# Attention, routed experts and FFN on one core: constants built behind the first pair's loads, attention rows stored pair by pair, and a newly searched order of steps

## The chip, the cores and the metric

The kernel runs on one core of a Trainium2 chip. The metric is the device time of one execution in microseconds (us), lower is better. A core has five engines with a queue each: TensorE (PE, its weight loads shown as PEld), VectorE (DVE), ScalarE (ACT), GpSimd (POOL) and SyncE (SP). An engine runs its own queue strictly in order and waits at an instruction until what that instruction needs is there. SP computes nothing: it only issues transfers (DMA) between the memory of the chip (DRAM here) and the core's memory, and an issue that waits holds up all later ones in its queue. ACT and POOL can issue transfers too. Matmul results go to PSUM, in banks of 128 x 512 numbers; tiles there and in the core's memory come from pools with a fixed number of buffers for each tag, so that a new tile may have to wait until an older one has been read.

## What is computed

```python
# q, k, v: 4 batches x 8 heads x 576 tokens x 64, float32
local = softmax(causal(q @ k.T / 8)) @ v
q_p = where(q > 0, q, exp(q) - 1) + 1
mem_out = (q_p @ M_prev) / (q_p @ z_prev + 1e-6)
g = 1 / (1 + exp(-beta))                       # one number for each head
x = (g * mem_out + (1 - g) * local)            # -> 2304 tokens x 512
...
e = argmax(x @ w_gate)                         # one expert of 8 for each token
y = softmax(x @ w_gate)[e] * sigmoid(x @ w_output_gate)[e] * (relu(x @ w1[e]) @ w2[e])
...
h = y @ w_in
out = (h - tanh(h)) @ w_out                    # 512 -> 2048 -> 512
```

## The kernel before, in words

The program has three stages, one after the other: attention, the routed experts (`run_slots`), and the FFN (`ffn`). The change touches the first stage and the point where it hands over to the second; the code of the other two is the same.

**Attention** works on 16 *pairs*: four batches `b` times four pairs of heads `hp`, numbered `n = 4b + hp`. One pair takes this course, and each step is one `add(...)` of the function `pair`:

- SP loads k (`kr`), q (`qr`) and v (`vr`, with the last 64 rows in `vt`), several transfers each. The last 64 rows of q and of k share one block of the tile `qr`.
- PE turns k and q over (`tk`, `tq`, `tt`), and ACT or DVE copies the results out of PSUM (`kt`, `qt`; DVE makes `qtt`).
- PE makes the scores of four blocks of query rows (`sc0` makes two of them, `sc2`, `sc3`, each with one matmul for each head), and of the last 64 rows of both heads together (`sct`, and `sdt` for its last 64 columns). DVE masks each block and takes its extreme (`mx`, `mxt`), ACT takes the exponential (`ex`, `ext`).
- PE turns the results over (`g0`, `g1`, `g2`, `ta`, `tb`), ACT or DVE copies them (`cp`, `ca`, `cb`) into `att`.
- Beside that, ACT, POOL and DVE make the memory branch: `qexp`, `qmin` (POOL), `phi`, `pz` (POOL, with `z`), `gn`, and after the sums are known `nrm` and `p` (POOL). PE turns `p` over (`tp`, `tpt`).
- PE multiplies with v (`av0`, `av1`, `av2`, 20 matmuls into `l`) and adds the memory part (`avM`, with `M`). The result is copied (`lt`), and one more matmul (`xo`, with the constant `w160`) turns it back and makes the columns for the experts' choice on the way. DVE scales it into `xb` (`xw`).

After the last pair of a batch, DVE sums the choice columns (`acc`), and the **router** (class `Router`) finds each token's expert in about thirty small steps; PE's part of it is the group `rank`, which writes `rp` from `ohb`. The rows of `xb` go to the DRAM table `xd` in five transfers (`putx`), the gate factors `sc` in two more (`puts`). In the second stage experts fetch their tokens from `xd` by index. After the third batch one expert's first slot is already fetched (`e_gather`) and turned over (`e_xt`), so that the second stage can begin at once.

**The order of work** is not written by hand. `Plan.add` collects all steps with a cost for each engine and a due time out of the table `DUE` (plus the pair's number times `PERIOD`). `Plan.order` walks through them: among the steps whose inputs are planned and whose buffers are free it takes the one due first, and with its model of costs gives it a time. The steps are emitted in that order, and since each engine runs in order, it is the order on every engine. If a step issues several instructions on several engines, all of them go in at that place, whether its cost names them or not.

**Constants.** Before the plan starts, `make_consts0`, `Router.__init__` and `make_consts` emit the identity `idf`, the masks, the gate factors from `beta` (`g`, `gt`, `ft`), `w160`, zeros for `att`, `vt` and `M`, and the router's small tables: for these POOL writes numbers (`iota`) into one shared buffer `io`, and DVE turns them into floats (`CAST`, L707, L723, L728), one after the other.

Of the kernel before, what the change touches and what calls it, by code (L numbers as in the profile page):

```python
# [57 lines left out]
def make_consts0(tc, pool):  # L58
    nc = tc.nc
    c = Consts()  # L60
    c.idf = pool.tile([P, P], F32, name="idf")
    make_identity(nc, c.idf)

    c.tri = pool.tile([P, P], BF16, name="tri")
    nc.gpsimd.memset(c.tri, 1.0)
    nc.gpsimd.affine_select(out=c.tri, in_=c.tri, compare_op=ALU.is_gt, fill=0.0,
                            base=0, pattern=[[1, P]], channel_multiplier=-1)
    c.ones = pool.tile([P, P], BF16, name="ones")
    nc.gpsimd.memset(c.ones, 1.0)
    return c  # L70


def make_consts(tc, c, pool, beta, w_gate, w_ogate):

    nc = tc.nc

    def tile1(name, shape, dt=F32):
        return pool.tile(shape, dt, bufs=1, name=name)


    c.cm = tile1("cm", [P, 512 + P])
# [8 lines left out]
    nc.gpsimd.memset(c.bm, 0.0)  # L90
    c.sel = tile1("sel", [P, P])
    for j in range(2):
        pr = slice(D * j, D * j + D)
        nc.gpsimd.memset(c.bm[pr, j:j + 1], 1.0)
        nc.vector.tensor_tensor(out=c.sel[:, pr], in0=c.idf[:, 0:D], in1=c.idf[:, D:P], op=ALU.add)


    g0, g, f = (tile1(n, [P, H]) for n in ("g0", "g", "f"))
    nc.sync.dma_start(g0, beta.unsqueeze(0).to_broadcast([P, H]))
# [9 lines left out]
    c.gt = tile1("gt", [P, NPAIR, NT, 2])  # L109
    c.ft = tile1("ft", [P, NPAIR, NT, 2])  # L110
# [4 lines left out]
    c.w160 = tile1("w160", [P, NPAIR, 2, 80])  # L115
# [28 lines left out]
class Plan:  # L144

# [37 lines left out]
    def order(self):  # L183
# [19 lines left out]
        while ready:  # L203
# [60 lines left out]
PERIOD = 23.73  # L264
ROUTE = 1.78
DUE = {
    "pz": (-91.5,), "qexp": (-84.8,), "qt": (-84.8,), "ptt": (-84.4,),
    "mx": (-59.4, -1.4, -5.0, -2.9, -31.8, -33.8, 16.5, -30.4), "ca": (-58.7, -10.0), "qmin": (-34.1,),
    "ex": (-33.6, 17.3, -4.6, 12.5, 16.0, -2.3, 26.1, 20.7), "loadq": (-30.6,), "consts": (-30.0,),
    "kt": (-26.7,), "loadk": (-22.3,), "qtt": (-11.6,), "sct": (-10.5,), "tp": (-10.5,), "phi": (-10.1,),  # L270
    "nrm": (-6.2,), "new": (-4.8,), "mxt": (-3.4,), "ktt": (-2.6,), "avM": (-1.5,), "mv": (0.7,), "tk": (0.7,),
# [5 lines left out]
}  # L277


def attention(tc, c, pl, ps, src, M_prev, z_prev, rt):  # L280
# [17 lines left out]
    def consts(b):  # L298
        def f(e):
            z = pl.tile([P, H * D], F32, tag="z", name=f"z_{b}")  # L300
            nc.sync.dma_start(z, z_prev[b].rearrange("h d -> (h d)").unsqueeze(0).to_broadcast([P, H * D]))
            state.z = {**getattr(state, "z", {}), b: z}
            for j in range(2):
                pr = slice(D * j, D * j + D)
                nc.sync.dma_start(c.M[b % 2][pr, :, pr], M_prev[b].rearrange("(n j) d e -> j d n e", j=2)[j])
        plan.add(b * NPAIR * PERIOD + DUE["consts"][0], f"consts_{b}", (("SP", 0.3),), f,
                 w=[f"z{b}", f"M{b % 2}"], new=[("z", f"z{b}")], lat=4.0)

    def pair(b, hp):
# [12 lines left out]
        def load(name):  # L322
# [13 lines left out]
            add("load" + name, (("SP", 0.4),), f, w=w, new=[(name + "r", K(name + "r"))], lat=5.0)  # L336
# [24 lines left out]
        add("gn", (("DVE", 1.2),), gn, r=[K("pz")], w=[K("gn")])  # L361
# [237 lines left out]
        add("xo", (("PE", 3 * mm(160) + 0.1),), xo(0), r=[K("lt/a"), K("lt/b")], w=[K("xo")], new=[("tr", K("xo"))])  # L599
# [14 lines left out]
        add("xw", (("DVE", 0.46),), xw(1), r=[K("l0"), K("r")], w=[f"xb{b % 2}/{hp}1"])  # L614

    def batch(b):
# [21 lines left out]
        for k, (t, name, f) in enumerate(sorted(rt.batch(b, accs.get, pl, ps), key=lambda x: x[0])):  # L638
# [5 lines left out]
            dur = {"hot": 1.7, "e_gather": 1.2, "e_sc0": 1.2, "e_sc1": 1.2, "e_xt0": 0.44, "e_xt1": 0.44, "e_list": 0.6}.get(nm, 0.25 if eng != "SP" else 0.5)  # L644
            if nm == "put":
                eng = "ACT" if b == B - 1 else eng
                plan.add(base + DUE["r"][0], f"{name}_{b}", ((eng, 0.4),), lambda e, f=f: f(), r=xs, w=[f"xd{b}"], lat=6.0)
                continue
            r, w, new = [prev], [f"R{b}_{k}"], []
# [25 lines left out]
class Router:  # L675
# [3 lines left out]
    def __init__(self, tc, c, pool, xd):  # L679
# [6 lines left out]
        self.rank = pool.tile([P, n], F32, name="rank")  # L686
        nc.gpsimd.memset(self.cs[:, 0, :], 0.0)
# [31 lines left out]
        self.pt = pool.tile([P, n, 2], F32, name="ptc")  # L719
# [56 lines left out]
    def batch(self, b, get, pl, ps):  # L776
# [896 lines left out]
```

## Time and profile before

| what | us |
|---|---|
| three runs | 1007.35, 1006.24, 1007.66 |
| median | 1007.35 |
| the profiled execution's own time | 1006.93 |
| its span in the profile | 1005.1 |
| PE busy | 929.8 (93%) |
| DVE busy | 816.2 (81%) |
| ACT busy | 660.3 (66%) |
| POOL busy | 128.5 (13%) |

The span is the time from the first to the last instruction of the profiled execution; 1.8 us of its own time lie around it. Shares of busy time are averages over three stages that have different limits, so the rows below are read by stage: attention runs to about 282 us, the experts from there to about 580, the FFN to the end. The granted clock of TensorE (PEclk) is a share of its full speed, so 1.00 is 2.4 GHz and 0.50 is 1.2 GHz.

### The profile page before, as it was taken

What the parts mean: (1) busy time and instruction counts of PE and PEld (TensorE: products, weight loads), DVE (VectorE), ACT (ScalarE), POOL (GpSimd) and SP (SyncE); (2) the same over time, 40 slices, a digit from 0 to 9 for tenths busy, and PEclk for the clock granted to TensorE, in tenths of its full rate; (3) what the DMA queues carried; (4) which work ended last, traced back from release to release, by engine and by line L of the source; (5) the groups of instructions that cost most, each with busy time, mean ns of one, the idle gap of its engine ahead of it and who ended that gap; (6) DMA issues with size and microseconds to landing.
All of it is one profiled execution on the core that took longest, in us unless ns stands there. A gap on an engine that the chain in (4) does not pass through costs nothing. (4 is left out here: it accounts for less than half of the span.)

```text
span 1005.1 us, 16594 instructions
## 1 busy us (share of the span) xinstructions
PE 929.8 (93%) x5661; PEld 760.2 (76%) x5661; DVE 816.2 (81%) x1901; ACT 660.3 (66%) x1448; POOL 128.5 (13%) x145
## 2 busy tenths in 40 slices
PE   3998998998959999999999979999999999999996
PEld 2565665665649998989989958777888788788885
DVE  4767675867659898998988869999888888888896
ACT  2777576776625667676687566767667666756684
POOL 4333222232221100001000000001000100100010
PEclk9999999999979999999999979999999999999999
DMA  5323324513176788798888410101000100100010
GB/s 115 79 53 72 89 46 83 124 32 77 35 215 213 250 280 268 256 297 248 276 289 283 135 44 22 43 1 43 1 0 1 43 1 1 43 1 0 4 41 21
DMA packets 138413, 103.60 MB, mean 103 GB/s; under 512 B 85072, under 2 KB 119888, under 8 KB 138320
## 3 DMA queue, kind: packets, MB, share of 16 engines
q1 hardware_dynamic: 130432, 90.70, 31.2%
q0 software_dynamic: 3200, 10.58, 3.2%
q10 hardware_dynamic: 4688, 1.18, 0.6%
q8 instruction: 46, 0.75, 0.3%
q14 instruction: 47, 0.39, 0.1%
HBM read 92.93 MB, written 9.51 MB: 102 GB/s over the span
## 5 line engine op out<-in xcount | busy, mean ns | idle before, releaser
L1440 PE MATMUL og<-wouth,fgl 128*128 128x512 f32 x288 | 115.4, 401 | 7.9 <-DVE fgl L1451 7.8
L1440 PE MATMUL og<-woutl,fgh 128*128 128x512 f32 x288 | 114.6, 398 | 0.0
L1440 PE MATMUL og<-wouth,fgh 128*128 128x512 f32 x288 | 113.4, 394 | 0.2
L1524 ACT ACTIVATE fu<-fph 128x512 f32<-128x512 f32 (+1 forms) x80 | 44.4, 555 | 105.4 <-PE fph L1491 77.6
L1491 PE MATMUL fph<-fxh,fwh 128*128 128x512 f32 (+1 forms) x256 | 94.2, 370 | 4.8 <-ACT fxh L50 4.8
L1491 PE MATMUL fph<-fxh,fwl 128*128 128x512 f32 (+1 forms) x256 | 93.5, 368 | 0.0
L1491 PE MATMUL fph<-fxl,fwh 128*128 128x512 f32 (+1 forms) x256 | 93.4, 367 | 0.0
L453 ACT ACTIVATE a<-a,nm 128x128 f32<-128x128 f32 (+3 forms) x128 | 72.6, 571 | 24.4 <-DVE nm L432 24.2
L1458 POOL DMA_INDIRECT out_dram<-ob,olist x18 | 18.9, 1048 | 459.8 <-ACT ob L1456 246.9
L1526 DVE SCALAR_TENSOR_TENSOR fs<-fs,fu 128x512 f32<-128x512 f32 (+1 forms) x80 | 50.9, 636 | 30.2 <-ACT fs L1525 29.8
L51 DVE TENSOR_TENSOR bl<-r,bh 128x512 fp32r<-128x512 f32 x96 | 64.5, 685 | 11.1 <-ACT bh L50 10.7
L1440 PEld LDWEIGHTS og<-wouth,fgl 128*128 128x128 f32 x288 | 54.2, 188 | 25.0 <-DVE fgl L1451 13.2
L1279 PE MATMUL y<-hh,bh 128*128 128x256 f32 x256 | 72.2, 282 | 0.0
L1279 PE MATMUL y<-hl,bh 128*128 128x256 f32 x256 | 71.6, 280 | 0.0
L1279 PE MATMUL y<-hh,bl 128*128 128x256 f32 x256 | 71.6, 280 | 0.0
L51 DVE TENSOR_TENSOR al<-r,ah 128x512 fp32r<-128x512 f32 x96 | 64.3, 684 | 0.1
L1440 PEld LDWEIGHTS og<-wouth,fgh 128*128 128x128 f32 x288 | 54.4, 189 | 12.6 <-ACT fgh L1446 1.5
L1440 PEld LDWEIGHTS og<-woutl,fgh 128*128 128x128 f32 x288 | 54.4, 189 | 12.0 <-DVE woutl L51 0.5
L432 DVE CUSTOM_DVE_ANT_0 a<-sc,cm 128x128 f32<-128x128 f32 (+3 forms) x128 | 55.5, 479 | 7.0 <-PE sc L412 6.9
L1537 DVE TENSOR_TENSOR ft<-fph,ft 128x512 f32<-128x512 f32 (+1 forms) x80 | 50.9, 636 | 11.6 <-ACT ft L1535 11.2
L1271 ACT ACTIVATE hh<-ph 128x256 fp32r<-128x256 f32 x64 | 24.6, 385 | 53.8 <-PE ph L1266 53.8
L1491 PEld LDWEIGHTS fph<-fxh,fwh 128*128 128x128 f32 x256 | 49.0, 192 | 14.1 <-ACT fxh L50 5.7
(372 smaller groups left out, 2825.2 us busy)
## 6 DMA issues: line engine op xcount, KB each, us to landing
r<-in_moe_w_dram SPq DMA_DIRECT2D x96, 512.0 KB, 5.0
d<-in_moe_w_in_dram SPq DMA_DIRECT2D x16, 512.0 KB, 4.6
d<-in_moe_w_out_dram SPq DMA_DIRECT2D x16, 512.0 KB, 4.4
qr<-in_q_dram SPq DMA_DIRECT2D x32, 128.0 KB, 2.7
kr<-in_k_dram SPq DMA_DIRECT2D x32, 128.0 KB, 2.6
vr<-in_v_dram SPq DMA_DIRECT2D x32, 128.0 KB, 2.6
r_e<-in_moe_w_dram SPq DMA_DIRECT2D x8, 512.0 KB, 5.8
xd<-xb SPq DMA_DIRECT2D x12, 256.0 KB, 4.2
```

The costliest lines, as they stand in the source:

```text
L51: nc.vector.tensor_tensor(out=lo, in0=src, in1=hi.bitcast(F32), op=ALU.subtract)
L432: nc.vector.tensor_tensor_reduce(out=y, in0=x, in1=mask, scale=-0.125, scalar=init, op0=ALU.add, op1=ALU.min, accum_out=out)
L453: nc.scalar.activation(a, a, AF.Exp, bias=s.nm[:, o:o + 1], scale=-1.0, accum_out=s.sum[:, i, j:j + 1])
L1271: nc.scalar.activation(hh, hv, AF.Relu)
L1279: nc.tensor.matmul(s.y[d // 2][:, d % 2, :], st[:, d * P:(d + 1) * P], mv, start=f == 0 and m == 0 and d % 2 == 0, stop=f == 7 and m == 2, ...
L1440: nc.tensor.matmul(og[ci][t], st[:, ts], mv, start=f == 0 and m == 0, stop=f == 15 and m == 2)
L1458: sc = nc.gpsimd.indirect_dma_start(out=out, out_offset=bass.IndirectOffsetOnAxis(ap=perm[:, i:i + 1], axis=0), in_=ob, in_offset=None).ins
L1491: nc.tensor.matmul(h, st[:, k, :], xp[ci, k][o], start=m == 0, stop=m == 11)
L1524: nc.scalar.activation(u, h, AF.Square)
L1526: nc.vector.scalar_tensor_tensor(out=s, in0=s, scalar=KA, in1=u, op0=ALU.add, op1=ALU.mult)
L1537: nc.vector.tensor_tensor(out=th, in0=h, in1=th, op=ALU.subtract)
```

## The change

- `make_consts` keeps what the first scores need. Four groups of constants become steps of the plan, with due times of their own (`DUE0`): `M` (zeros for the memory tiles), `zeros` (for `att` and `vt`), `gates` (from `beta`) and `w160`. The router's tables, with `tri` and `ones`, become a fifth step, `laterrt`, which calls `Router.consts`; its cost in the plan is 3.5 us of POOL. `beta` is loaded from ACT's queue instead of SP's.
- `z` and `M` of a batch are loaded by two steps instead of one.
- The rows of `xb` are stored by a step `put` of each pair: two transfers for the first 512 rows (one for each head), two for the last 64, all from SP's queue. The five transfers at the end of a batch go, those of the last batch (which ACT issued) among them.
- The plan's costs for loads change: 2.1, 1.15 and 1.75 us of SP for q, k and v where all had 0.4, and 3.0 us to land where it was 5.0. Its rule for PSUM banks changes by a line: any use of a bank now counts against all earlier ones from other engines.
- The due times are new.

```diff
 def make_consts0(tc, pool):
     c.tri = pool.tile([P, P], BF16, name="tri")
-    nc.gpsimd.memset(c.tri, 1.0)
-    nc.gpsimd.affine_select(out=c.tri, in_=c.tri, compare_op=ALU.is_gt, fill=0.0,
-                            base=0, pattern=[[1, P]], channel_multiplier=-1)
...
 def make_consts(tc, c, pool, beta, w_gate, w_ogate):
...
+    nc.scalar.dma_start(g0, beta.unsqueeze(0).to_broadcast([P, H]))
...
+    c.later = {
+        "M": lambda: memories(nc, c),
+        "zeros": lambda: zeros(nc, c),
+        "gates": lambda: gates(nc, c, g0, g, f),
+        "w160": lambda: columns(nc, c, w_gate, w_ogate),
+    }
...
 class Plan:
                 for k in touch[i][0] | touch[i][1]:
-                    t = max([t] + [u for g, u in wrote.get(k, {}).items() if g != e])
-                for k in touch[i][1]:
-                    t = max([t] + [u for g, u in read.get(k, {}).items() if g != e])
+                    t = max([t] + [u for d in (wrote, read) for g, u in d.get(k, {}).items() if g != e])
...
-PERIOD = 23.73
+PERIOD = 19.44
...
+DUE0 = {"constsM": 33.9, "constsz": 16.3, "laterM": -165.5, "latergates": 6.8, "laterrt": 17.1, "laterw160": -25.5, "laterzeros": 23.6}
...
 def attention(tc, c, pl, ps, src, M_prev, z_prev, rt):
+    for name, e, dur in (("M", "POOL", 1.1), ("zeros", "POOL", 0.9), ("gates", "DVE", 2.3), ("w160", "DVE", 0.9)):
+        plan.add(DUE0["later" + name], f"later{name}_0", ((e, dur),), lambda e, f=c.later[name]: f(), w=[f"later/{name}"],
+                 lat=6.0 if name == "w160" else 0.0)
+    plan.add(DUE0["laterrt"], "laterrt_0", (("POOL", 3.5),), lambda e: rt.consts(), w=["later/rt"], lat=1.0)
...
-            add("load" + name, (("SP", 0.4),), f, w=w, new=[(name + "r", K(name + "r"))], lat=5.0)
+            add("load" + name, (("SP", {"q": 2.1, "k": 1.15, "v": 1.75}[name]),), f, w=w, new=[(name + "r", K(name + "r"))], lat=3.0)
...
+        def put(e):
+            for r0, rows, x in ((b * S, 512, xb[:, 0:4, h0:h0 + 2, 0:D]), (b * S + 512, D, xb[0:D, 4:5, h0:h0 + 2, 0:D])):
+                for j in range(2):
+                    nc.sync.dma_start(rt.xd[r0:r0 + rows, h0 * D + j * D:h0 * D + j * D + D].rearrange("(t p) d -> p t d", t=x.shape[1]), x[:, :, j, :])
+        add("put", (("SP", 1.6),), put, r=[f"xb{b % 2}/{hp}0", f"xb{b % 2}/{hp}1"], w=[f"xd{b}{hp}"], lat=3.0)
...
 class Router:
-        at(0, "put")(lambda: putx(nc.scalar if b == B - 1 else nc.sync, get(b)[0]))
```

**Place 1, the head, queues of SP and DVE.** SP before, from its first transfer:

```order
L99 DMA g_157<-in_beta_dram 128x8
L329 DMA qr_215<-in_q_dram 128x4x64 x2
L333 DMA qr_215<-in_q_dram 64x2x64
L333 DMA qr_215<-in_k_dram 64x2x64
L301 DMA z_223<-in_z_prev_dram 128x512
L122 DMA w_181<-in_moe_w_gate_dram 64x4x8
L122 DMA w_181<-in_moe_w_output_gate_dram 64x4x8
L122 DMA w_181<-in_moe_w_gate_dram 64x4x8
L122 DMA w_181<-in_moe_w_output_gate_dram 64x4x8
L305 DMA M_205<-in_M_prev_dram 64x4x64 x2
L329 DMA kr_227<-in_k_dram 128x4x64 x2
L329 DMA qr_233<-in_q_dram 128x4x64 x2
```

and now (`w` is `w160`):

```order
L352 DMA qr_130<-in_q_dram 128x4x64 x2
L356 DMA qr_130<-in_q_dram 64x2x64
L356 DMA qr_130<-in_k_dram 64x2x64
L135 DMA w_109<-in_moe_w_gate_dram 64x4x8
L135 DMA w_109<-in_moe_w_output_gate_dram 64x4x8
L135 DMA w_109<-in_moe_w_gate_dram 64x4x8
L135 DMA w_109<-in_moe_w_output_gate_dram 64x4x8
L352 DMA kr_155<-in_k_dram 128x4x64 x2
L352 DMA qr_165<-in_q_dram 128x4x64 x2
```

The first k (`kr`) has lost `beta`, `z` and `M` ahead of it; `w160` still stands there. On DVE the router's tables stood ahead of the first block of scores (`a` and `nm` are written by `mx`):

```order
L707 CAST ish<-ish_i 128x20
L120 COPY w_181<-idf 64x64 x5
L707 CAST pos<-pos_i 128x20
L707 CAST thr<-thr_i 128x18
L347 SCALAR_TENSOR_TENSOR ph_220<-qr_215,ph_220 128x640
L723 CAST ptc<-io_t 128x40
L724 MEMSET ptc 64x4x2
L728 CAST ir<-io_r 128x128
L394 TENSOR_TENSOR qtt_265<-tt_263,bm 128x128
L432 ISA a_0_244,nm_241<-sc_0_268,cm 128x128
```

and now they stand between the last block of pair 0 and the first of pair 1:

```order
L383 RECIPROCAL gn_278<-gn_278 128x10
L735 CAST ie<-io_e 128x8
L738 TENSOR_SCALAR rev<-ie 128x8
L743 TENSOR_TENSOR le<-ie 128x64
L751 CAST num<-num_i 128x20
L751 CAST num_302<-num_i 128x20
L751 CAST ish<-ish_i 128x20
L751 CAST pos<-pos_i 128x20
L751 CAST thr<-thr_i 128x18
L766 CAST ptc<-io_t 128x40
L767 MEMSET ptc 64x4x2
L771 CAST ir<-io_r 128x128
```

The two instructions of DVE that follow are `phi` of pair 1, which needs POOL's `qmin` of pair 1, queued on POOL behind the router's tables, and the first `mx` of pair 1.

**Place 2, PE in the middle of a pair (here pair 5's scores).** Before, `sct` and then `sdt` (the matmul with 64 columns) followed `sc2`:

```order
L412 MATMUL sc_5_1080<-kt_1005,qt_1012 128x384
L412 MATMUL sc_5_1081<-kt_1005,qt_1012 128x384
L425 MATMUL sct_1086<-kt_1005,qtt_1038 128x512
L427 MATMUL sc_5_1081<-kt_1005,qtt_1038 128x64
L476 MATMUL g_4_1095<-idf,a_1_810 128x128 x4
```

Now `sdt` comes ahead of `sct`, and `tk` of the next pair has moved here:

```order
L435 MATMUL sc_5_1097<-kt_938,qt_868 128x384
L435 MATMUL sc_5_1098<-kt_938,qt_868 128x384
L450 MATMUL sc_5_1098<-kt_938,qtt_995 128x64
L448 MATMUL sct_1103<-kt_938,qtt_995 128x512
L391 MATMUL tk_1109<-idf,kr_1030 128x128 x4
```

The matmul with 64 columns writes into the bank of `sc2`'s second half; it now stands ahead of DVE's reading of that half instead of behind it.

**Place 3, PE at the turn of a batch (batch 0).** Before, the router's group `rp` (twelve instructions, of which the last two are shown) was followed by `xo`:

```order
L862 LDWEIGHTS ones
L862 MATMUL rp_1225<-ohb_1215,ones 128x8
L597 MATMUL xo_1243<-w_181,lt_1240 128x160 x3
L597 MATMUL l_4_1115<-w_181,lt_1240 128x160 x2
L377 MATMUL tt_1255<-idf,qr_965 128x128
```

Now the group (its first three instructions are shown) stands right behind the last matmuls of a pair with M, and `tq`, `ta` and `sc0` of other pairs follow it:

```order
L603 MATMUL l_5_1308<-pt_1316,M_116 128x128
L604 MATMUL l_5_1309<-pt_1316,M_116 128x448
L887 LDWEIGHTS tri
L887 MATMUL rp_1412<-ohb_1402,tri 128x40
L888 LDWEIGHTS ones
```

So `rp` no longer stands ahead of an `xo` that waits for `lt`, and waits for `ohb` at another point of DVE's work.

## Rows read from the trace of the kernel before

**Rows 1.** Busy time from the first to the last `av` of attention, by engine.

```profile
core 0: us, PE busy (x) PEld busy (x) DVE busy (x) ACT busy (x) POOL busy (x), PEclk, DMA share, GB/s
38.80:275.80 237.00, 219.25 (x1500) 147.45 (x1498) 164.64 (x621) 165.58 (x470) 67.69 (x51) 0.99 0.32 67
```

**Rows 2.** Timeline of the head: start us, us, engine, line, operation [idle before <-releaser].

```profile
3.64 0.17 DVE L101 TENSOR_SCALAR g<-g 128x8 f32<-128x8 f32 x1 [3.64 <-ACT g L100]
5.74 0.16 DVE L691 CAST ie<-io_e 128x8 f32<-128x8 int32 x1
6.23 0.61 DVE L707 CAST num<-num_i 128x20 f32<-128x20 int32 x1
6.83 0.60 SPq L122 DMA_DIRECT2D w<-in_moe_w_gate_dram  x1
10.82 1.15 SPq L329 DMA_DIRECT2D kr<-in_k_dram  x2
14.24 1.09 PE L368 MATMUL tk<-idf,kr 128*128 128x128 f32 x4 [14.24 <-DMA kr<-in_k_dram]
16.75 1.80 POOL L346 TENSOR_SCALAR ph<-ph 128x640 f32<-128x640 f32 x1 [1.75 <-ACT ph L344]
17.68 4.03 PE L412 MATMUL sc<-kt,qt 64*128 64x128 f32 x12 [1.28 <-ACT qt L288]
```

**Rows 3.** Timeline of PE, attention: starts of `av` (L566), and one `sdt`.

```profile
38.85 2.81 PE L566 MATMUL l<-att,vr 128*64 128x448 f32 x20
50.27 0.44 PE L427 MATMUL sc<-kt,qtt 128*128 128x64 f32 x2 [0.35 <-DVE nm L432]
53.55 2.81 PE L566 MATMUL l<-att,vr 128*64 128x448 f32 x20
100.42 4.56 PE L566 MATMUL l<-att,vr 128*64 128x448 f32 x17 [2.74 <-DMA vr<-in_v_dram]
264.21 2.81 PE L566 MATMUL l<-att,vr 128*64 128x448 f32 x20
275.81 2.81 PE L566 MATMUL l<-att,vr 128*64 128x448 f32 x20
```

**Rows 4.** Waits, 0 to 290 us: engine line, releaser: us, times, longest.

```profile
PE l L566 <- DMA vr<-in_v_dram: 7.0, 4, 2.7
PE xo L597 <- ACT lt L288: 5.3, 4, 1.5
PE sc L427 <- DVE nm L432: 5.1, 14, 0.4
```

**Rows 5.** SP's queue ahead of the late v.

```profile
89.97 5.15 SPq L848 DMA_DIRECT2D xd<-xb  x5
97.74 1.14 SPq L329 DMA_DIRECT2D vr<-in_v_dram  x2
```

**Rows 6.** A stretch after that wait, columns as in rows 1.

```profile
102.00:104.00 2.00, 2.00 (x11) 1.30 (x9) 0.95 (x7) 0.00 (x0) 0.18 (x1) 0.50 0.06 12
```

**Rows 7.** Timeline from attention to the experts.

```profile
274.44 0.60 PE L978 MATMUL e_xt<-idf,e_xg 128*128 128x128 f32 x4
282.35 0.40 SPq L1211 DMA_DIRECT2D r_e<-in_moe_w_dram  x1
282.50 8.19 ACTq L848 DMA_DIRECT2D xd<-xb  x5
282.90 1.26 DVE L630 TENSOR_REDUCE acc<-xb 128x64 f32<-128x512 f32 x2
285.84 0.22 PE L858 MATMUL rp<-ohb,tri 128*128 128x40 bf16 x1 [3.52 <-DVE ohb L811]
291.46 0.58 PE L1266 MATMUL ph_e<-xh_first,ah_e 128*128 128x256 f32 x1 [5.13 <-ACT ah_e L1225]
```

**Rows 8.** Transfers by line: count, KB each, median us to landing.

```profile
xd<-xb SPq DMA_DIRECT2D x12, 256.0 KB, 4.2
r_e<-in_moe_w_dram SPq DMA_DIRECT2D x8, 512.0 KB, 5.8
```

More of the change, by code (lines that the diff above doesn't have):

```diff
@@ L90, in make_consts, with gates @@
     nc.gpsimd.memset(c.bm, 0.0)
+    for j in range(2):
+        nc.gpsimd.memset(c.bm[D * j:D * j + D, j:j + 1], 1.0)
     c.sel = tile1("sel", [P, P])
-    for j in range(2):
[L93 to L99, printed above, removed]
+    g0, g, f = (tile1(n, [P, H]) for n in ("g0", "g", "f"))
+    nc.scalar.dma_start(g0, beta.unsqueeze(0).to_broadcast([P, H]))
+    c.gt = tile1("gt", [P, NPAIR, NT, 2])
+    c.ft = tile1("ft", [P, NPAIR, NT, 2])
+    c.w160 = tile1("w160", [P, NPAIR, 2, 80])
+    c.at = [tile1(f"att{i}", [P, 2, 1600]) for i in range(2)]
+    c.vt = [tile1(f"vt{i}", [P, P]) for i in range(3)]
+    c.M = [tile1(f"M{i}", [P, NPAIR, P]) for i in range(2)]
+    c.xb = [tile1(f"xb{i}", [P, NT, H, 80]) for i in range(2)]
+    c.later = {
[4 more added lines that the diff above has]
+    }
+def gates(nc, c, g0, g, f):
+    for j in range(2):
+        nc.vector.tensor_tensor(out=c.sel[:, D * j:D * j + D], in0=c.idf[:, 0:D], in1=c.idf[:, D:P], op=ALU.add)
     nc.scalar.activation(g0, g0, AF.Exp, scale=-1.0)
@@ L262 @@
 QORDER = (1, 3, 2, 0)
-PERIOD = 23.73
-ROUTE = 1.78
+PERIOD = 19.44
+ROUTE = 1.48
 DUE = {
[L267 to L271, printed above, removed]
[5 rows of a table removed]
+    "mx": (-371.1, -38.4, -63.2, -4.7, -23.8, -10.4, -17.1, -329.2), "kt": (-356.8,), "nrm": (-319.8,),
+    "phi": (-319.7,), "qtt": (-218.6,), "pt": (-193.0,), "ptt": (-174.7,),
+    "ex": (-97.7, -29.7, -360.9, -178.0, 9.4, 9.1, -54.4, -78.3), "lt": (-66.1, -9.5), "mxt": (-65.1,),
+    "cp": (-60.8, -194.3, -30.0, -48.9, -29.0), "tpt": (-49.1,), "sdt": (-48.6,), "qt": (-47.4,),
+    "new": (-45.7,), "sm": (-45.7,), "loadq": (-36.0,), "consts": (-30.0,), "qexp": (-29.5,), "loadk": (-20.7,),
[6 rows of a table added]
 }
+DUE0 = {"constsM": 33.9, "constsz": 16.3, "laterM": -165.5, "latergates": 6.8, "laterrt": 17.1, "laterw160": -25.5, "laterzeros": 23.6}
 def attention(tc, c, pl, ps, src, M_prev, z_prev, rt):
@@ L360, in gn @@
             nc.vector.reciprocal(s.gn, s.gn)
-        add("gn", (("DVE", 1.2),), gn, r=[K("pz")], w=[K("gn")])
+        add("gn", (("DVE", 1.2),), gn, r=[K("pz"), "later/gates"], w=[K("gn")])
         def tr(name, x):
@@ L567, in f @@
                                              start=kb == 0, stop=False, skip_group_check=True)
+            zs = ["later/zeros"] if name == "av2" else []
             parts = {"av0": ["00", "01", "t0"], "av1": ["10", "11", "t0", "t1"], "av2": ["2", "t1", "t2"]}[name]
             wide = {"av0": 576, "av1": 640, "av2": 384}[name]
-            add(name, (("PE", mm(wide) + 0.02),), f, mode="col", r=[f"{AK}/{x}" for x in parts] + [K("vr"), f"vt{n % 3}"] + ([K("l1/p")] if first else []),
+            add(name, (("PE", mm(wide) + 0.02),), f, mode="col", r=[f"{AK}/{x}" for x in parts] + [K("vr"), f"vt{n % 3}"] + ([K("l1/p")] if first else []) + zs,
                 w=[K("l0")] + ([K("l1/o")] if first else []))
@@ L598, in xo @@
             return f
-        add("xo", (("PE", 3 * mm(160) + 0.1),), xo(0), r=[K("lt/a"), K("lt/b")], w=[K("xo")], new=[("tr", K("xo"))])
+        add("xo", (("PE", 3 * mm(160) + 0.1),), xo(0), r=[K("lt/a"), K("lt/b"), "later/w160"], w=[K("xo")], new=[("tr", K("xo"))])
         add("xo", (("PE", 2 * mm(160)),), xo(1), r=[K("lt/a"), K("lt/b")], w=[K("l0")])
@@ L643, in batch @@
             eng = kinds.get(nm) or ("PE" if nm.startswith("e_xt") else "ACT" if nm.startswith("e_xh") else "POOL" if nm.startswith("e_sc") else "DVE")
[L644 to L649, printed above, removed]
+            dur = {"hot": 1.7, "e_gather": 1.2, "e_sc0": 1.2, "e_sc1": 1.2, "e_xt0": 0.44, "e_xt1": 0.44, "e_list": 0.6}.get(nm, 0.25 if eng != "SP" else 1.0)
+            r, w, new = [prev, "later/rt"], [f"R{b}_{k}"], []
             if nm == "puts":
@@ L686, in __init__, with consts @@
         self.rank = pool.tile([P, n], F32, name="rank")
+        self.a = pool.tile([P, n, P], BF16, name="oneh")
+        self.early = pool.tile([P, n], F32, name="early")
+        self.epos = pool.tile([P, n], F32, name="epos")
+        self.eeq = pool.tile([P, n, 2], BF16, name="eeq")
+        self.pt = pool.tile([P, n, 2], F32, name="ptc")
+        self.rhi = pool.tile([P, n], F32, name="rhi")
+        self.rlo = pool.tile([P, n], F32, name="rlo")
+    def consts(self):
+        tc, c, pool = self.tc, self.c, self.pool
+        nc = tc.nc
+        n = B * NT
+        nc.gpsimd.memset(c.tri, 1.0)
+        nc.gpsimd.affine_select(out=c.tri, in_=c.tri, compare_op=ALU.is_gt, fill=0.0,
+                                base=0, pattern=[[1, P]], channel_multiplier=-1)
+        nc.gpsimd.memset(c.ones, 1.0)
         nc.gpsimd.memset(self.cs[:, 0, :], 0.0)
```

34 lines of the change are left out of this document (10 added, 24 removed), and 11 rows, old and new, of the table DUE.

## The prediction

> **What bounds the kernel now.** I read the busy time by stage first, then the timeline of PE through attention, the waits, the queue of SP, and the two ends of the stage. Between the first and the last `av` PE is busy 219 of 237 us, DVE and ACT some 165 each [rows 1]: PE sets the pace there, so what counts is what holds PE up or slows it. `av` starts are the clock hand. From pair 0 to pair 1 it takes 14.70 us (38.85 to 53.55), and the last step, which has no next pair beside it, 11.60 (264.21 to 275.81) [rows 3]. Fourteen steps of 14.70 and one of 11.60 make 217.4 us; the sixteen `av` lie 236.96 us apart. So 19.6 us have been lost on the way, and the waits name most of it: 7.0 us for v in four waits, and 5.3 for `lt` in four, of which three cost 1.5 each [rows 4]. Twice PE comes back from the wait for v at half clock: the stretch behind 102 us has a granted clock of 0.50, 1.2 GHz instead of 2.4 [rows 6], and 17 matmuls of `av` take 4.56 us there where 20 take 2.81 [rows 3], 1.75 lost each time. Together 7.0 + 4.5 + 3.5 = 15.0; the rest is mostly the router's own work on PE. Every step of 14.70 also holds a wait of 0.35 us of `sdt` for DVE [rows 3, 4].
>
> Why is v late? It stands in SP's queue behind the five stores of a batch, which are issued only when the last pair of the batch is in `xb`, at 89.97, and take 5.15 us; q follows, and v goes out at 97.74, just ahead of the `av` that wants it [rows 5].
>
> At the head, PE's first matmul waits until 14.24 for k, issued at 10.82 [rows 2]. At the far end, `xb` is full at 282.9 and the experts' first matmul comes at 291.46, held by ACT, which spent 8.19 us issuing the last batch's stores [rows 7]. All that follows shifts with that matmul; nothing in the change touches it.
>
> **The change part by part**, as differences to the profiled execution.
>
> *Stores by pair.* Now SP issues put, k, q, v in turn, and v is wanted by the next `av`. The put is free when `xo` of the pair before is scaled, about when an `av` starts. No row shows stores of this shape; the nearest are the two halves of k, alike in shape and size, 1.15 us for two [rows 2], so four stores cost some 2.4; at ACT's price, 8.19 for five [rows 7], they would cost 6.5. Add 1.15 for k, 2.6 for q (95.12 to 97.74 [rows 5]), 1.9 for v at q's price for each transfer, and 2.3 from the end of k's issue to its first use (11.97 to 14.24 [rows 2]): 10.4 us of a period of 14.4, a margin of 4. At ACT's price it is used up, not exceeded. At the turn of a batch `z`, `M` and the two stores of `sc` join the queue, and the latter wait for DVE's router steps; I estimate a margin between 1 and 2 us there. So the waits for v go: −7.0, and the half-clock stretches with them: −3.5. If the margin fails at the turns, nothing of the 10.5 is won.
>
> The rows show that queue as issue after issue with landings beside them: two transfers of k leave within 1.15 us [rows 2], a store of 256 KB lands in 4.2 [rows 8] while others are issued. The Trainium skill (DMA: Bandwidth & Descriptors, Anatomy of one DMA, and the rule under Measured) speaks against this part: it gives a DMA a fixed cost of about 2.0 us and asks for batches of 1 MiB or more, and the change makes 64 stores out of 20. By that figure 44 more stores would add 88 us if they passed one at a time, and none if they overlap.
>
> *rp moved [place 3].* The three waits of 1.5 us for `lt` behind `rp` go, −4.5. Instead `rp` waits for `ohb`. The chain from `acc` to `rp` took 2.94 us (282.90 to 285.84 [rows 7]); beside it PE has the 2.81 us of `av` and the matmuls with M, but DVE has the two blocks of `sc3` to do first. Between 0 and 2.94 each time I take 1.2, since most of the chain is covered: +3.6. Behind `rp` on PE everything waits, `tq` first.
>
> *sdt ahead of sct [place 2].* It no longer waits for DVE to finish with its bank; what DVE reads afterwards is ordered behind it. 14 × 0.35 = −4.9. The next thing that could be late is `tpt`, which needs POOL's `p`; it has moved behind `tk` and gets more room. The first `tk` and `tq` of a pair now run most of a period ahead of the scores; that costs PE nothing and takes two copies off its heels.
>
> *Last step.* The two turns `e_xt` move out of it, behind the last `av`; with 0.60 a group less overlap [rows 7] some −1.0.
>
> *Head.* q of pair 0 is first. `w160`'s four transfers still precede k, and wait for POOL's memset: before, they left from 6.83, and k four microseconds later [rows 2]. POOL now has some 3.4 us of memsets ahead of them, so I put them at 4.2, k at 6.9, PE's `tk` 3.4 us later at 10.3. `tq` is then done already, so the scores, 3.44 us behind `tk` before, come some 1.9 behind it, at 12.2 instead of 17.68: 5.5 us won. But between pair 0 and pair 1 DVE now has the gate factors (3.64 to 5.74, 2.1 us) and the router's tables, handed over through one buffer, 0.49 us for each (5.74 to 6.23 [rows 2]) with eight or nine of them 4.2. Behind these stand POOL's memsets (0.4) and its 1.80 for `qmin` [rows 2], then `phi`, then the first `mx` of pair 1, on which PE's second `sc2` waits for a bank. That is 8.5 us of new work in line. If all of it is hidden, −5.5; if none, +3.0; as it stands in the chain that pair 1 waits for, I lean to that end: +1.0 at the first `av`. PE stands some 7 us idle before it and comes back at half clock, which is in this figure.
>
> *Far end.* ACT is free, but the loads of the experts' first weights now stand behind the last pair's put: `xb` full at 282.9 plus half a microsecond for the `e_xt` ahead of `xo`, plus 2.4 of stores, 285.8 instead of 282.35. With 5.8 to land [rows 8] and 0.6 to convert that is 292.2 against 291.46; with a batch's stores no longer beside them they may land sooner. I take +0.5, between −2 and +2.
>
> Sum: −7.0 − 3.5 − 4.5 + 3.6 − 4.9 − 1.0 + 1.0 + 0.5 = **−15.8 us**. The profiled execution took 1006.93 with a span of 1005.1, 0.42 under the median of 1007.35; the same difference from the median gives **991.6 us**. Its own bounds: −27 (no wait at `rp`, head −5.5, far end −2) to −8 (head +3, `rp` 2.94, far end +2).
>
> **The rivals.**
>
> 1. *The head pays too.* DVE's new work lies in gaps; the first `av` comes 4 to 5.5 us sooner. For it: DVE has gaps, busy 165 of 237 us later on [rows 1]. Against: all of it stands in one queue ahead of pair 1. −15.8 − 6 gives about **986**.
> 2. *v is late again at the turns.* The put, `z`, `M` and the stores of `sc` ahead of it leave a margin of 1 to 2 us that my estimate can't vouch for. With three waits of 2 and half clock after two, 9.5 us come back: **1001**. For it: the waits of before sit just there.
> 3. *Slower: each store holds SP until it has landed.* Place: SP's queue, between put and v, at every pair. At 2.6 us each (between half of a 256 KB store's 4.2 [rows 8] and the whole) the way to v takes 18.4 us, 4 more than the period, 14 times: 56 us more, **1048**. It decides from 1.1 us late a pair, that is 1.9 us a store, on; above it the change is slower. Against it: the two transfers of k within 1.15 us [rows 2]. At the Trainium skill's 2.0 us a store (the page above) it would be 16.0 us, 1.6 late each time, and the change would end near 1014.
> 4. *It does not do what it says.* The order comes out of a model that gives the router's tables no time on DVE; if its steady period is no better either, the head's loss and the far end's eat the gain, 1005 to 1009.
>
> **How the numbers follow.** Forecast (987 to 998) 0.58; rival 1 (981 to 987) 0.14; rival 2 (998 to 1004) 0.15; rival 3 0.05; rival 4 0.06; better still 0.02. A measurement of this kernel tells about 0.2%, 2 us, from no change. Rival 3 and a third of rival 4 are slower: 0.07; the same third within 2 us, with a sliver of rival 2: 0.04; faster 0.89. The range 981 to 1001 takes in forecast, rival 1 and half of rival 2.
>
> **What would show it.** `av` starts 14.35 us apart in the middle; no wait of `av` for v and no clock of 0.50 between 60 and 250 us; no wait of L450 for DVE; `rp` waiting about a microsecond for `ohb`; the first score near 12 us but the first `av` near 40; the experts' first matmul within 1 us of 9 us after `xb` is full. It would be wrong if `av` still waits for v, if the steps stay at 14.7 or above, or if the first `av` comes at 34 or at 44.

## The result and the profile after

The changed kernel takes **982.79 us** (median of four runs, 981.97 to 983.69) against 1006.8 of the kernel before beside it (four runs): a ratio of 0.9764, 95% interval 0.9746 to 0.9782, 24.0 us less. The forecast of 991.6 was 9 us too high and its range, 981 to 1001, holds the time. The profiled execution took 983.37 with a span of 981.5, 23.6 under the span before. Its pieces, forecast beside measured:

| piece | forecast | measured | after, us |
|---|---|---|---|
| first `av` | +1.0 | +2.98 | 38.85 to 41.83 |
| first to last `av` | −17.3 | −23.33 | 236.96 to 213.63 |
| last `av` to the experts' first matmul | +0.5 | −1.20 | 15.65 to 14.45 |
| from there to the end | 0 | −2.05 | 713.64 to 711.59 |

Between the first and the last `av`, columns as in [rows 1], PE now does its work in 23 us less and has 4.5 idle instead of 18:

```profile
41.80:255.40 213.60, 209.06 (x1483) 143.92 (x1481) 157.33 (x623) 159.24 (x460) 66.13 (x47) 0.99 0.35 79
```

The waits of PE, 60 to 240 us, hold no line for v and none of `sdt` for DVE any more; one group is left:

```profile
PE rp L887 <- DVE ohb L847: 1.8, 3, 0.6
```

The steps from `av` to `av` are 14.12 us, 15.09 and 15.08 at two turns of a batch, and 14.09 in the last. PE's timeline through a middle pair has the order of place 2, with no idle time:

```profile
70.07 2.81 PE L589 MATMUL l<-att,vr 128*64 128x448 f32 x20
...
77.72 0.92 PE L435 MATMUL sc<-kt,qt 64*128 64x384 f32 x4
78.56 0.43 PE L450 MATMUL sc<-kt,qtt 128*128 128x64 f32 x2
78.84 1.08 PE L448 MATMUL sct<-kt,qtt 128*128 128x512 f32 x2
79.75 0.60 PE L391 MATMUL tk<-idf,kr 128*128 128x128 f32 x4
```

At a turn, where v went out at 97.74 just ahead of its `av` [rows 5], SP now issues it at 122.22 for an `av` at 127.52:

```profile
112.05 2.14 SPq L643 DMA_DIRECT2D xd<-xb  x4
114.29 0.53 SPq L317 DMA_DIRECT2D z<-in_z_prev_dram  x1
114.92 1.33 SPq L323 DMA_DIRECT2D M<-in_M_prev_dram  x2
116.30 1.15 SPq L352 DMA_DIRECT2D kr<-in_k_dram  x2
118.71 0.37 SPq L877 DMA_DIRECT2D xd<-sc  x1
...
122.22 1.09 SPq L352 DMA_DIRECT2D vr<-in_v_dram  x2
127.52 2.81 PE L589 MATMUL l<-att,vr 128*64 128x448 f32 x20
```

The last step is worse than before, 14.09 where it was 11.60 [rows 3]. PE's timeline has it waiting for the router's list:

```profile
250.59 0.53 PE L944 MATMUL e_pp<-e_bm,oneh 128*128 128x4 bf16 x15 [1.63 <-DVE e_bm L953]
```

and behind that wait the clock is down (busy time of a stretch, columns as in [rows 1]):

```profile
253.00:255.00 2.00, 2.00 (x11) 2.00 (x10) 0.61 (x1) 0.81 (x3) 0.96 (x2) 0.51 0.55 146
```

At the head (answering to [rows 2]) k and the first score come 4.2 and 5.3 us sooner, and more than that is lost between pair 0 and pair 1. DVE converts the router's tables one by one and mostly waits for POOL (three of eleven rows are shown); POOL's `qmin` stands behind them, `phi` behind that, and PE waits 3.91 us and resumes at half clock (the last row, with columns as in [rows 1], has the granted clock at 0.50):

```profile
6.64 1.15 SPq L352 DMA_DIRECT2D kr<-in_k_dram  x2
12.37 4.03 PE L435 MATMUL sc<-kt,qt 64*128 64x128 f32 x12
25.32 0.11 DVE L735 CAST ie<-io_e 128x8 f32<-128x8 int32 x1
26.27 0.18 DVE L751 CAST num<-num_i 128x20 f32<-128x20 int32 x1 [0.33 <-POOL num_i L749]
29.16 0.23 DVE L771 CAST ir<-io_r 128x128 f32<-128x128 int32 x1 [0.21 <-POOL io_r L769]
29.56 1.81 POOL L369 TENSOR_SCALAR ph<-ph 128x640 f32<-128x640 f32 x1
31.40 0.83 DVE L370 SCALAR_TENSOR_TENSOR ph<-qr,ph 128x640 f32<-128x640 f32 x1 [2.01 <-POOL ph L369]
32.83 1.64 PE L435 MATMUL sc<-kt,qt 64*128 64x384 f32 x2 [3.91 <-DVE nm L455]
...
34.00:36.00 2.00, 2.00 (x5) 1.08 (x5) 1.66 (x5) 0.80 (x3) 2.00 (x6) 0.50 0.49 110
```

At the far end (answering to [rows 7]) the first weights leave behind the last stores, but they land in some 3.4 us instead of 5.8 [rows 8]:

```profile
256.25 9.28 SPq L643 DMA_DIRECT2D xd<-xb  x8
265.79 0.40 SPq L1240 DMA_DIRECT2D r_e<-in_moe_w_dram  x1
269.24 0.62 ACT L1254 CAST ah_e<-r_e 128x512 fp32r<-128x512 f32 x1 [5.89 <-DMA r_e<-in_moe_w_dram]
269.91 0.58 PE L1295 MATMUL ph_e<-xh_first,ah_e 128*128 128x256 f32 x1 [2.49 <-ACT ah_e L1254]
```

### The profile page after: what moved, and what is told of

Its sections match the earlier page's. It is cut to its first block, busy times and chain, and to the rows that moved or that the text cites. A ratio compares the mean times of both kernels' runs of the same rounds, so it can differ in the third digit from the quotient of the medians.

```text
span 981.5 us, 16678 instructions
## 1 busy us (share of the span) xinstructions
PE 924.2 (94%) x5661; PEld 759.2 (77%) x5661; DVE 807.3 (82%) x1908; ACT 655.7 (67%) x1441; POOL 128.3 (13%) x145
## 5 line engine op out<-in xcount | busy, mean ns | idle before, releaser
L455 DVE CUSTOM_DVE_ANT_0 a<-sc,cm 128x128 f32<-128x128 f32 (+3 forms) x128 | 57.5, 487 | 8.9 <-PE sc L435 8.6
L1469 PEld LDWEIGHTS og<-wouth,fgh 128*128 128x128 f32 x288 | 54.3, 189 | 12.7 <-ACT fgh L1475 1.4
```

The costliest lines, as they stand in the source:

```text
L455: nc.vector.tensor_tensor_reduce(out=y, in0=x, in1=mask, scale=-0.125, scalar=init, op0=ALU.add, op1=ALU.min, accum_out=out)
L1469: nc.tensor.matmul(og[ci][t], st[:, ts], mv, start=f == 0 and m == 0, stop=f == 15 and m == 2)
```

## The experiments

Times are medians of 5 to 12 runs; the ratio is to the kernel before, run beside them (1006.1, 1006.2 and 1004.9 in the three groups). Of long lines in the edits only the changed entry is shown.

### Is it the stores that let v be on time, or the order?

**stores_by_batch**, the changed kernel with the old stores:

```diff
+            if hp < NPAIR - 1:
+                return
+            for t in range(NT):
...
+                nc.sync.dma_start(rt.xd[r0:r0 + rows, 0:DM].rearrange("p (h d) -> p h d", d=D), xb[0:rows, t, :, 0:D])
```

> The changed kernel with the rows of a batch stored at its end again, by five transfers from SP's queue after its last pair; every other instruction keeps its place. Theory A, the gain at the turns comes from storing pair by pair: v waits again at three turns, 2 to 2.7 us each, and half clock follows twice, 10 us back, 993. Theory B, the new order alone leaves room enough: at the turns v is issued at 122.22 for an av at 127.52 and lands in 2.3, a margin of 3.0 us, and five stores (5.15) are 3.0 longer than four (2.14), so each wait for v is 0 to 1 us, 0 to 3 in all. By either theory the loads of the first expert leave 3 us later at the far end: A 996, B 986 to 989.

985.14 us, ratio 0.9787 (0.9764 to 0.9811). No `av` waits for v, and the turns take 15.09 us as in the changed kernel. SP's queue shows the five stores in a turn:

```profile
97.25 3.92 SPq L646 DMA_DIRECT2D xd<-xb  x5
101.22 1.53 SPq L352 DMA_DIRECT2D kr<-in_k_dram  x2
105.23 1.09 SPq L352 DMA_DIRECT2D vr<-in_v_dram  x2
```

v goes out only 1.4 us later than in the changed kernel (105.23 against 103.82), for an `av` due at 112. Theory B: the new order has the room. What stores by pair bring here is at the far end, 14.45 instead of 18.03 us. The time differs by less than these 3.6 us, since the last step of stores_by_batch runs at full clock, 12.47 us instead of 14.09.

**old_order_pair_stores**, the kernel before with stores by pair:

```diff
+    "put": (40.4,)
...
+        add("put", (("SP", 1.6),), put, r=[f"xb{b % 2}/{hp}0", f"xb{b % 2}/{hp}1"], w=[f"xd{b}{hp}"], lat=3.0)
...
```

> The kernel before, with its own order, costs and constants, and only the stores changed: four transfers after each pair instead of five after each batch. Theory A: the put shortens SP's queue ahead of v at a turn from 5.15 to 2.14 us, v leaves 3 us sooner where it was up to 2.74 late, so the waits for v (7.0) and the half clock behind them (3.5) go, and the far end is within 2 us: 994 to 998. Theory B, the order is what makes v early: a put ahead of every q and v makes other pairs late as well, waits for v stay above 4 us in all, 1002 or more. By either theory the steps stay at 14.70 us, since sct still stands ahead of sdt.

1015.71 us, ratio 1.0097 (1.0077 to 1.0117): slower than the kernel before. PE waits for v seven times, in six pairs, instead of four times (the waits of PE):

```profile
PE l L566 <- DMA vr<-in_v_dram: 11.1, 7, 3.6
```

in the middle of batches as well (the timeline of SP's queue and PE):

```profile
45.43 2.16 SPq L619 DMA_DIRECT2D xd<-xb  x4
47.69 1.08 SPq L329 DMA_DIRECT2D qr<-in_q_dram  x2
...
52.19 1.15 SPq L329 DMA_DIRECT2D vr<-in_v_dram  x2
55.07 4.56 PE L566 MATMUL l<-att,vr 128*64 128x448 f32 x19 [2.17 <-DMA vr<-in_v_dram]
```

The four stores take 2.16 us, no more than forecast. But in the old order the put can leave only 5 to 7.5 us ahead of the `av` that the v behind it is for, as due at 14.70 us a step (45.43 for an `av` due at 52.8, 64.50 for one due at 69.8); in the changed kernel it leaves 14 to 15.5 us ahead (112.05 for 127.52). More is lost inside `av` than ahead of it: the loads of v into PE as weights wait for v too (0.76 us at 71.90), and in thirteen pairs `av` up to M takes 3.5 to 5.0 us instead of 2.85, at half clock in some and at full clock in others. That is 15.1 us in all, where the kernel before loses 5.8.

**put_behind_v** moves the put alone:

```diff
-    "put": (40.4,)
+    "put": (75.0,)
```

> The kernel before with its own order and stores by pair, as in the run old_order_pair_stores, but the put stands behind the next v and k in SP's queue instead of ahead of q and v. Theory, what a store costs is its place: ahead of v it holds the queue until xb is scaled, behind v it holds nothing that is wanted soon. Then no pair waits for v for the put's sake, the waits for v (7.0) and the half clock (3.5) of the kernel before go too, since the five stores at the turn are gone, and the time is 994 to 998, some 20 under old_order_pair_stores. Rival, the number of stores is what costs (four for each pair instead of five for each batch): v stays late wherever the put stands, over 1008.

1000.91 us, ratio 0.9957 (0.9942 to 0.9972), 15 under the run before it with the same number of stores. The pairs within a batch are back at 14.70 without a wait for v. Two waits of 2.9 remain, at turns (`PE l L566 <- DMA vr<-in_v_dram: 5.8, 2, 2.9`), where the stores of `sc` wait for the router and hold q and v in the same way (issued at 104.36, v at 112.23). So the place in the queue is what costs, and the expectation missed that `sc` has such a place too.

### What shortened the step from 14.70 to 14.12?

**sct_first**:

```diff
-    "sct": (-13.4,)
+    "sct": (-48.7,)
```

> The changed kernel with sct ahead of sdt again in each pair, nothing else moved. Theory wait only: 0.35 us for each of 15 steps comes back, the step is 14.47 and the time 988. Theory wait and lost overlap: behind sdt the next matmul starts 0.91 us after sct's start, where sct ahead of a wait took its full 1.13, so a wait costs 0.35 + 0.22 = 0.57; the step is 14.69 and the time 991. Rival: the swap is not what shortened the step, 14.12 stays, 983.

981.64 us, ratio 0.9760 (0.9740 to 0.9781), steps of 14.06. The rival holds: which of the two matmuls goes first does not matter.

**read_first**, the same PE order, and DVE reads sc2 first as before:

```diff
-    "mx": (-371.1, -38.4, -63.2, -4.7, -23.8, -10.4, -17.1, -329.2)
+    "mx": (-371.1, -38.4, -63.2, -4.7, -23.8, -70.0, -17.1, -329.2)
```

> The changed kernel with sct ahead of sdt, and besides with DVE's reading of the second half of sc2 moved ahead of its reading of sct, as the order of the kernel before had it; PE's order is that of the run sct_first. Theory, what shortened the step is when DVE reads that bank, not which matmul goes first: sdt writes into the bank and must wait until it is read, 0.35 us a pair, and with the overlap lost behind it the step is 14.65 to 14.70 instead of 14.06, 9 us in all, 990 to 991. Rival, the step is short for another reason (the moved tk and tq, fewer copies on their heels): no wait of sdt or one that is hidden, steps under 14.2, 981 to 983.

985.18 us, ratio 0.9793 (0.9780 to 0.9806). Middle steps stay at 14.07, so it isn't the order of the readings either. DVE comes to sc2 in time, and waits for PE instead of PE for DVE, since no copy out of `ta` stands ahead of it here:

```profile
149.35 0.29 DVE L302 COPY att<-tb 64x128 f32<-64x128 f32 x1
149.86 0.56 DVE L455 CUSTOM_DVE_ANT_0 a<-sc,cm 128x384 f32<-128x384 f32 x1 [0.22 <-PE sc L435]
```

Only at three steps, where DVE is late, does `sdt` wait 1.5 us.

**ca_behind**, on the kernel before. There DVE stood at a copy that waited for ACT's copy into the same tile, and came to sc2 late:

```profile
49.32 0.42 DVE L288 COPY att<-ta 128x256 f32<-128x256 f32 x1 [0.70 <-ACT att L288]
49.66 0.55 DVE L432 CUSTOM_DVE_ANT_0 a<-sc,cm 128x384 f32<-128x384 f32 x1
50.27 0.44 PE L427 MATMUL sc<-kt,qtt 128*128 128x64 f32 x2 [0.35 <-DVE nm L432]
```

```diff
-    "ca": (-58.7, -10.0)
+    "ca": (-58.7, 31.3)
```

> The kernel before with one due time changed: the copy of the second half of ta into att, which stood on DVE ahead of its reading of sc2, comes behind sdt, where the plan gives it to ACT. PE's order is untouched, sct still goes first. Theory, the 0.35 us that sdt waited came from this copy: DVE stood 0.70 us at it, waiting for ACT's copy into the same tile, and read sc2 so much later. Without it DVE reads sc2 in time, sdt does not wait, the step is 14.70 - 0.35 - 0.22 = 14.13 as in the changed kernel, 15 times, and the time 997 to 998. Rival, DVE is late by more than that, or the copy on ACT delays an exponential that PE wants: the step stays over 14.5, 1003 to 1007.

1001.80 us, ratio 0.9965 (0.9950 to 0.9980). The undisturbed steps are 14.03 to 14.09, as in the changed kernel, and PE runs through:

```profile
50.07 1.12 PE L425 MATMUL sct<-kt,qtt 128*128 128x512 f32 x2
51.03 0.33 PE L427 MATMUL sc<-kt,qtt 128*128 128x64 f32 x2
51.20 1.04 PE L476 MATMUL g<-idf,a 128*128 128x128 f32 x8
```

That is the cause of the step, and its price is 0.6 us a pair for a wait of 0.35: ahead of the wait `sct` runs out its 1.13 us, without it the next matmul starts after 0.91 to 0.96. The time fell by 3.1 us (2 to 5), not 8: only six steps are undisturbed, and the first `av` comes 1.3 us later (40.13). The eight others, from 14.6 to 19.6 us, take 136.3 us where they took 137.2, since PE comes sooner to an `av` whose v comes no sooner; the waits for v grew from 7.0 to 8.4:

```profile
PE l L566 <- DMA vr<-in_v_dram: 8.4, 4, 3.2
```

### The head

**tables_early**:

```diff
-"laterrt": 17.1
+"laterrt": -25.4
```

> The changed kernel with the router's tables moved to the front, behind the constant w160 and ahead of qmin of pair 0, where DVE stands idle from 5.05 to 11.6 us and POOL from 4.0 to 7.0. Theory C, the tables between pair 0 and 1 are what costs the head its 3 us: DVE's phi of pair 1, at 31.40 now, can start when POOL's qmin is done, some 4 to 6 us sooner, the half clock between 26 and 40 us shrinks, the first av comes at 35 to 37 instead of 41.83, and the time is 976 to 978. Rival: something else of the head is late next (exponentials, k or q of pair 1), the first av moves by under 2 us, 981.

973.25 us, ratio 0.9678 (0.9658 to 0.9698). The first `av` comes at 32.50, 9.3 us sooner, more than theory C had: `phi` starts at 25.41, six us sooner, and without the wait of 3.91 the matmuls ahead of `av` are not at half clock:

```profile
25.41 0.83 DVE L370 SCALAR_TENSOR_TENSOR ph<-qr,ph 128x640 f32<-128x640 f32 x1
32.50 2.81 PE L589 MATMUL l<-att,vr 128*64 128x448 f32 x20
```

**own_buffers**, the tables in their place, without the shared buffer (one of four such edits is shown):

```diff
-            t = pool.tile([P, n], I32, tag="io", bufs=1, name=name + "_i")
+            t = pool.tile([P, n], I32, name=name + "_i")
```

> The changed kernel, order and all, with a buffer of its own for each of the router's integer tables instead of one shared. Theory, much of the 4.1 us that the tables hold DVE is the handing over: POOL waits for DVE to read, DVE for POOL to write, 2.2 us of waits of 0.21 to 0.59; with own buffers POOL writes while DVE does other work and DVE's block takes some 1.9, so phi of pair 1 and the first av come 2 to 4 us sooner: 979 to 981. Rival, qmin of pair 1 behind the tables on POOL (1.80) sets phi's start, not DVE's block, and POOL is no sooner: under 1 us, 982 to 983.

975.14 us, ratio 0.9706 (0.9679 to 0.9732), first `av` at 36.79. POOL writes all tables by 21.5 and goes on to `qmin`, and DVE's block has no waits:

```profile
21.91 1.83 POOL L369 TENSOR_SCALAR ph<-ph 128x640 f32<-128x640 f32 x1
26.09 0.11 DVE L735 CAST ie<-io_e 128x8 f32<-128x8 int32 x1
27.18 0.23 DVE L771 CAST ir<-io_r 128x128 f32<-128x128 int32 x1
27.32 0.82 DVE L370 SCALAR_TENSOR_TENSOR ph<-qr,ph 128x640 f32<-128x640 f32 x1
```

Handing over cost most of it: the block falls from 4.1 to 1.3 us, and `phi` no longer waits for POOL. Of the 8.3 us by which the profiled span fell, 5.0 are the head. Some 1.6 more are the last step, 12.48 us at full clock, and 1.7 lie behind the experts' first matmul, where one stretch that has half clock in the changed kernel (granted clock 0.66 between 575 and 580 us) runs at full clock here; neither was touched.

**best0** and **last_put_pool** try other ends.

```diff
-"laterrt": 17.1, "laterw160": -25.5
+"laterrt": -19.9, "laterw160": -20.0
+            if nm == "e_list":
+                at = max(at, 14 * PERIOD + 47.0)
```

> The run tables_early with two more edits: the four transfers of w160 stand behind the first k instead of ahead of it, and the group e_list of the router is placed behind the last xo, ahead of the last av, where PE waited 1.63 us for it. Theory: k leaves at 3.3 instead of 6.64, PE's scores start near 9 instead of 12.4 and the first av comes at 29 to 30 instead of 32.5; the wait of 1.63 goes; 973.25 - 3 - 1.6 = 968 to 969. Rival: behind k the q of pair 1, now later, or ACT's copies set the pace, and e_list's late start holds the experts' first matmul: 971 to 973.

970.74 us, ratio 0.9652 (0.9637 to 0.9667). The rival's account fits: PE's scores wait behind `tq` of pair 1, which waits 2.36 us for its q, and the first `av` comes at 33.42; the last step falls to 11.15, but the later list holds `e_xt`, and `rp` behind it.

```diff
-                    nc.sync.dma_start(
+                    (nc.gpsimd if n == B * NPAIR - 1 else nc.sync).dma_start(
```

> The changed kernel with the four stores of the very last pair issued from POOL's queue instead of SP's. Theory, at the far end the first weights wait in SP's queue behind that put: they leave some 2.5 to 3 us sooner (263 instead of 265.79), the first conversion follows, and the experts' first matmul comes 2 to 2.5 us sooner, held then by rp: far end 12 to 12.5 instead of 14.45, 980.5. Rival, the weights wait for the memory that xb gives back, or POOL's issue holds its share of the first conversion: nothing gained, 983, or up to 3 us slower, 986.

982.14 us, ratio 0.9765 (0.9753 to 0.9778). The weights leave at 260.68 and the far end is 12.80 us, as theorized, but what follows is 713.69 us instead of 711.59: a later matmul of the first expert waits 1.97 us for its weights (`al_e`) where the longest such wait was 0.89, PE runs at half clock once more behind it (granted clock 0.50 between 277 and 280 us), and the gain is gone.

**best5**, the version that beats both: `gates`, `w160` and tables in the idle time of the head, buffers of their own, `tq` of pair 1 behind the first scores.

```diff
-"latergates": 6.8, "laterrt": 17.1, "laterw160": -25.5
+"latergates": -19.85, "laterrt": -19.9, "laterw160": -20.0
+            plan.add(base + DUE[name][k] + (1.9 if name == "tq" and n == 1 else 0.0), f"{name}_{n}", engines, fn, r, w, new, lat, mode)
```

(with the edits of own_buffers and last_put_pool)

> The changed kernel with the head put in order and the far end eased: k of pair 0 ahead of w160; the router's tables in buffers of their own and the gates behind w160, in the time in which DVE and POOL are idle; tq of pair 1 behind the first scores instead of ahead of them, since its q lands at 10.4; the last pair's stores from POOL. Theory, scores start at 8.8 to 9.3 instead of 12.4 and nothing stands between pair 0 and pair 1 on DVE: the first av at 28 to 30 (32.5 in the run tables_early), the far end 12.8 instead of 14.5: 967 to 970. Rival, exponentials on ACT or z, which lands at 17, set the pace of pair 1: first av at 31 to 33, 971 to 973.

970.11 us, ratio 0.9650 (0.9623 to 0.9677), 12.7 under the changed kernel:

```profile
8.37 1.66 PE L435 MATMUL sc<-kt,qt 64*128 64x128 f32 x8 [0.46 <-ACT kt L302]
29.45 2.81 PE L589 MATMUL l<-att,vr 128*64 128x448 f32 x20
```

The head came out as its theory had it. The total is no lower than best0's: the last step, without best0's edit of `e_list`, is at half clock again (14.05), and the POOL stores give their gain back.

## Why the prediction was right or wrong

The time fell within the range, but in part by luck: the two largest parts, v with its half clock and `sdt`, came for other reasons than I gave, and misses of some 2 to 3.5 us stand on both sides.

- **v, −7.0 and −3.5 of half clock.** Both went; the margin worked out for the new queue was there (v issued 5.3 us ahead of its `av` at a turn). But the step "stores by pair, so the waits for v go" failed as a cause. In the new order five stores a batch cause no wait (stores_by_batch), and in the old one stores by pair cause more (old_order_pair_stores). I had priced the new queue rightly and credited the stores with what the place of q, k and v in it does: in the changed order `xo` comes most of a period after its `av` (the put leaves 13.7 us behind it, 98.31 to 112.05), and the loads have the rest of the next period.
- **Half clock was mis-sized.** I compared `av`'s first rows alone (4.56 against 2.81). With the rows on `vt` up to M, that turn takes 5.30 us (100.42 to 105.72) against 2.85 now (70.07 to 72.92): 2.45, not 1.75. The second such turn takes 4.89, 2.04 more, so the two turns lost 4.5 and not 3.5. At the other two waits `av` takes 3.33 and 3.71 us at full clock (granted 1.00), another 1.3 that I had not counted, while its weight loads wait for the rest of v (0.30 and 0.68 us):

```profile
165.76 4.58 PE L566 MATMUL l<-att,vr 128*64 128x448 f32 x19 [2.18 <-DMA vr<-in_v_dram]
184.85 3.02 PE L566 MATMUL l<-att,vr 128*64 128x448 f32 x19 [0.46 <-DMA vr<-in_v_dram]
231.18 2.97 PE L566 MATMUL l<-att,vr 128*64 128x448 f32 x17 [1.67 <-DMA vr<-in_v_dram]
```

- **"The rest is mostly the router's own work on PE"**, 4.6 us that I left in, was wrong. Of the 4.6, 2.3 is the slow `av` above and 0.6 a wait of `xo` for a copy of DVE (`lt`), which leaves 1.7. In the changed kernel a full turn is 0.97 us longer than a step, of which 0.60 is the wait of `rp`: the router's matmuls cost 0.37 a turn.
- **rp, −4.5 and +3.6.** The waits for `lt` went; `rp` waits 0.6 three times, 1.8 instead of 3.6.
- **sdt ahead of sct, −4.9.** The wait went, and the step fell by 0.58 instead of 0.35, 8.1 us in 14. The step named was wrong: the swap does nothing, the copy ahead of DVE's reading was the cause (ca_behind). The size was short of the overlap lost at a wait.
- **Last step, −1.0.** It came to +2.5: `e_pp` waits 1.63 for DVE, 3.6 us behind a wait of 1.10 for ACT, and the stretch behind it runs at 1.2 GHz. I had no term for either. The step differs from kernel to kernel with the same PE work: 14.05 to 14.23 us with half clock (the changed kernel, sct_first, last_put_pool, best5), 12.47 and 12.48 without (stores_by_batch, tables_early, own_buffers), and 13.44 in read_first, which has it behind a first wait of 0.52. So the clock is 1.6 of the 2.5; why it fell in some and not in others stays open.
- **Head, +1.0.** +2.98, at the end of its bounds that I called likelier. The total came out so, the terms did not. Without the tables (tables_early) `phi` starts 6.0 us sooner, near the 6.4 of tables, memsets and `qmin`, but the first `av` 9.3: the other 3.3 go with the half clock, which I had named without a number. Of the 2.1 of the gate factors, still in place there, nothing shows: from the first score to the first `av` it takes 20.3 us (12.24 to 32.50), where the kernel before takes 21.2.
- **Far end, +0.5.** −1.2: the loads left later, as forecast, and landed faster.
- **After the experts' first matmul, 0.** −2.05. Nothing there was changed, and the kernels with the new order and SP's stores scatter from 709.8 to 712.2 in this piece, those with the old order from 712.8 to 713.6. In own_buffers, the lowest, it is a stretch of half clock less; why the others differ stays open.
- **The sum's bounds**, −27 and −8, come to −28.4 and −7.1 from the terms named. Nothing hangs on it; the profiled execution fell by 23.6.

Rival 3 fell on its price: four stores take 2.14 us of SP's queue, 0.54 each, where 1.9 would have decided. The Trainium skill (DMA: Bandwidth & Descriptors, Anatomy of one DMA) gives the fixed cost of about 2.0 us for a transfer that GpSimd issues, and puts most of it down to completion and not to setup. The traces show it, if it is there, beside other work and not in SP's queue, so it was no price for this rival. The Trainium skill's rule to batch (the same page, under Measured) was no guide to the sign here: with the same number of small stores the old order ran at 1015.7 or 1000.9, by their place in the queue.

## What to carry to other kernels

A transfer that waits for its data holds every load behind it in its queue, so ask of a store where it stands and when its data is ready, before how many there are. A small wait can cost more than its idle time on an engine whose instructions overlap (0.6 us for 0.35 here), and its cause may be a copy that the waited-for engine made first: look one instruction further back. And constants handed from one engine to another through one buffer can cost more in waits than in work (here 2.8 of 4.1 us) when they stand between two pairs.

## What the runs showed of the hardware

PE ran at 1.2 GHz behind idle times of 1.10 and 1.63 us (granted clock 0.51 between 253 and 255 us), and in last_put_pool behind 0.84 and 1.97 us (0.50 between 277 and 280 us); stores_by_batch, tables_early and own_buffers had the first two waits as well (1.09 and 1.63) and stayed at 2.4 GHz.

Four stores issued by POOL took 2.73 us, and by SP 2.14. The five of ACT that had taken 8.19 [rows 7] give no price for ACT: one by one they took from 0.41 to 2.49 us, and the fifteen of the same kind on SP in the kernel before from 0.36 to 2.36. What makes the long ones long is not shown.
